# Key weight blocks 2 to 5 of the first stage, each loaded in two or more transfers cut along the partitions

## The chip, the cores and the metric

The kernel runs on one core of one Trainium2 chip. The metric is the device time of one execution in microseconds (us); the time of a kernel is the median of its runs. Engines are named as the profile names them: PE is TensorE (PEld its weight loads), DVE is VectorE, ACT is ScalarE, POOL is GpSimd, SP is SyncE, which here only issues transfers.

## The reference: what is computed

A transformer block with adaptive layer norm, linear attention of 32 heads and a SwiGLU feed-forward part. There are 2048 rows of 1024 features in bf16; the feed-forward width is 3584.

```python
mod = (_silu(c) @ w_mod).reshape(c.shape[0], 6, 1, -1)      # sa, ca, ga, sb, cb, gb
h = _layernorm(x) * (1 + ca) + sa
q, k, v = split(h @ wqkv)                                   # 32 heads of 32
pq, pk = phi(q), phi(k)                                     # where(t > 0, t + 1, exp(t)) + 1e-6
o = (pq @ (pk^T v)) / (pq @ sum(pk) + 1e-6)                 # per head
x = x + ga * (o @ wo)
h = _layernorm(x) * (1 + cb) + sb
x = x + gb * ((silu(h @ w_gate) * (h @ w_up)) @ w_down)
```

## The kernel before

The 2048 rows are worked in four chunks of 512, each chunk four tiles of 128 rows. A contraction over 1024 features is eight matmuls, one for each block of 128 features; the block is numbered `cc`, 0 to 7. The order of the instructions is written out by hand (`manual_schedule`), so what stands here is the order in which each engine's queue gets its work.

The change lies in the **first stage**, in which nothing is yet on the chip. Chunk 0 is normalized and transposed into `M4`, the vectors `sa` and `ca` of the modulation are computed, and the keys of chunk 0 are computed: eight groups (four row tiles by two halves of 512 columns), each of which adds up eight blocks in a bank of PSUM of its own. All this waits on its weights, and the order of the loads and the order of the matmuls are made for each other:

- The loads all go through SP's queue, in this order: four tiles of x (`load_x`, L137); the modulation weights for feature blocks 0 and 1 (`load_wme(0, ...)`, L144, two transfers); key weight blocks 0 and 1 (`load_wk(0, 2)`, L147); modulation weights for blocks 2 to 4 (four transfers); key blocks 2, 3, 4, one transfer each (256 KB: 128 partitions with one row of 2 KB each); modulation weights for blocks 5 to 7 (four transfers); key block 5; key blocks 6 and 7 in one transfer of 512 KB. After them come the value and query weights (`load_cols`, L150) and the x tiles 4 to 7. ACT's queue holds only the 2 KB of `c` here.
- Transfers are counted on eight completion semaphores, reused in turn, so an issue waits until the transfer eight before it has landed.
- PE runs block by block over all groups (`kblk`, with `kmm` at L273, and `kmm7` at L387 for the eighth group, whose bank it shares with the modulation), so that each weight block is used by eight groups once it has landed. Between them are the modulation's matmuls (`mod_mm`, L372, one column each), and `warm` and `fill` (L197, L382), matmuls on zeros that do no work of the reference.
- Once a phase of the modulation is complete (`mod_finish`, L378), DVE scales and shifts the feature blocks of that phase (`modulate`, L255), which PE then uses as weights.
- For blocks 5, 6 and 7 the order turns: PE goes group by group, with blocks 5, 6, 7 of each, and the finished group is evacuated (`k_evac`, ACT L268 and DVE L269, L270).

After the first stage come the value groups of chunk 0 (L288), the queries (L296), the key-value products (L305), the later chunks, the attention output and the feed-forward part (L561, L567, L586), all of which are streams of matmuls that share the five banks in turn.

Of the kernel before, what the change touches and what calls it, by code (L numbers as in the profile page):

```python
# [21 lines left out]
def kernel(  # L22
# [13 lines left out]
    nc = tc.nc  # L36
    P = nc.NUM_PARTITIONS
    _, S, D = A_x.shape
# [23 lines left out]
    wqkv_v = A_wqkv.rearrange("(c p) n -> p c n", p=P)  # L62
# [24 lines left out]
    def view(region, off, shape, dtype=BF16):  # L87
        n = 1
        for s_ in shape:
            n *= s_  # L90
        w = n * (2 if dtype == F32 else 1)
        ap = region[:, off:off + w]
        if dtype == F32:
            ap = ap.bitcast(F32)
        if len(shape) == 2:
            ap = ap.rearrange("p (a b) -> p a b", a=shape[0])
        elif len(shape) == 3:
            ap = ap.rearrange("p (a b c) -> p a b c", a=shape[0], b=shape[1])
        return ap

    wk = view(M12, 0, [DC, D])
# [39 lines left out]
    def load_wme(p, j0, j1):  # L141
        for base in (D, 0):
            s_ = slice(base + PH[p][0] * P, base + PH[p][1] * P)
            nc.sync.dma_start(out=wme[:, j0:j1, s_], in_=wm_v[:, j0:j1, s_])  # L144

    def load_wk(c0, c1):
        nc.sync.dma_start(out=wk[:, c0:c1, :], in_=wqkv_v[:, c0:c1, D:2 * D])  # L147

    def load_cols(dst, base, h):
        nc.sync.dma_start(out=dst[:, :, h * NB:(h + 1) * NB],  # L150
# [2 lines left out]
    for st in range(STC):  # L153
        load_x(st)
    load_wme(0, 0, DC)
    load_wk(0, 2)
    load_wme(1, 0, 4)
    load_wme(1, 4, 8)
    load_wk(2, 3)
    load_wk(3, 4)  # L160
    load_wk(4, 5)
    load_wme(2, 0, 4)
    load_wme(2, 4, 8)
    load_wk(5, 6)
    load_wk(6, 8)


# [577 lines left out]
```

## Time and profile before

| | |
|---|---|
| median of 7 runs | 838.6 us (837.83 to 840.85) |
| profiled execution | 840.85 us, of which the span from the first to the last instruction is 838.8 us |
| granted TensorE clock over the span | 0.998 |
| PE busy | 833.5 us (99% of the span) |
| DVE, ACT, POOL busy | 350.4, 151.6, 80.1 us |
| DMA | 129.41 MB, mean 154 GB/s |
| DMA in the first 12 us, in 12.04 to 20.95, in 20.95 to 26.68 | 272, 342, 357 GB/s |

All durations come from one profiled execution. Matmuls are pipelined: the profile shows 379 ns for one of 512 columns, but in a stream one starts every 0.216 us (64 in 13.81 us). A time "from issue to landing" counts from the issuing instruction's start to the last of the transfer's completions. In lists of waits and chains a name such as `PE bank L273` is engine, tile written and line; `DMA M<-in_A_wqkv_dram` is a transfer from that input to the region of SBUF called M.

### The profile page before, as it was taken

What the parts mean: (1) busy time and instruction counts of PE and PEld (TensorE: products, weight loads), DVE (VectorE), ACT (ScalarE), POOL (GpSimd) and SP (SyncE); (2) the same over time, 40 slices, a digit from 0 to 9 for tenths busy, and PEclk for the clock granted to TensorE, in tenths of its full rate; (3) what the DMA queues carried; (4) which work ended last, traced back from release to release, by engine and by line L of the source; (5) the groups of instructions that cost most, each with busy time, mean ns of one, the idle gap of its engine ahead of it and who ended that gap; (6) DMA issues with size and microseconds to landing.
All of it is one profiled execution on the core that took longest, in us unless ns stands there. A gap on an engine that the chain in (4) does not pass through costs nothing.

```text
span 838.8 us, 10625 instructions
## 1 busy us (share of the span) xinstructions
PE 833.5 (99%) x4232; PEld 390.6 (47%) x4232; DVE 350.4 (42%) x653; ACT 151.6 (18%) x288; POOL 80.1 (10%) x149
## 2 busy tenths in 40 slices
PE   9999999999999999999999999999999999999998
PEld 5444444544444444444444444444444444444445
DVE  5658888788655655344552111111101211111101
ACT  4335533323211111111110001111000111100000
POOL 2124210022122323100000000000000000000000
PEclk9999999999999999999999999999999999999999
DMA  9985879056499898998884215555322555211220
GB/s 302 300 178 102 161 140 250 17 151 135 126 226 226 217 203 226 249 284 238 251 247 136 76 70 150 151 152 153 106 72 84 156 155 153 76 36 46 76 70 26
DMA packets 230545, 129.41 MB, mean 154 GB/s; under 512 B 87648, under 2 KB 216672, under 8 KB 230496
## 3 DMA queue, kind: packets, MB, share of 16 engines
q1 hardware_dynamic: 180144, 97.01, 42.4%
q10 hardware_dynamic: 48048, 23.34, 12.8%
q0 software_dynamic: 2304, 8.39, 2.6%
q8 instruction: 33, 0.54, 0.3%
q14 instruction: 16, 0.13, 0.1%
HBM read 95.42 MB, written 12.58 MB: 129 GB/s over the span
## 4 chain that ended last, share of the span: by engine, by line
PE 96%; DMA 2%; SPq 1%; issue 0%; DVE 0%
PE bank L586 23%; PE bank L567 23%; PE bank L561 23%; PE bank L288 7%; PE bank L518 7%; PE bank L296 7%; PE bank L273 6%; PE bank L491 1%; DMA M<-in_w_mod_dram 1%; PE bank L305 1%; DMA M<-in_A_wqkv_dram 1%; SPq L147 1%; SPq L144 0%; SPq L137 0%; PE bank L387 0%
## 5 line engine op out<-in xcount | busy, mean ns | idle before, releaser
L567 PE MATMUL bank<-M,M 128*128 128x512 bf16 x896 | 211.7, 379 | 0.0
L561 PE MATMUL bank<-M,M 128*128 128x512 bf16 x896 | 211.6, 379 | 0.0
L569 DVE TENSOR_TENSOR M<-bank,e 128x512 bf16<-128x512 f32 x112 | 77.4, 691 | 250.4 <-PE bank L567 246.0
L586 PE MATMUL bank<-M,M 128*128 128x512 bf16 (+2 forms) x728 | 148.0, 363 | 0.0
L564 ACT ACTIVATE e<-bank 128x512 f32<-128x512 f32 x112 | 66.8, 597 | 439.6 <-PE bank L561 403.5
L586 PEld LDWEIGHTS <-M 128*128 128x128 bf16 x952 | 90.9, 98 | 102.9
L567 PEld LDWEIGHTS <-M 128*128 128x128 bf16 x896 | 87.6, 98 | 105.8
L561 PEld LDWEIGHTS <-M 128*128 128x128 bf16 x896 | 87.3, 98 | 103.9
L589 DVE TENSOR_TENSOR M<-bank,M 128x512 bf16<-128x512 f32 (+2 forms) x34 | 22.4, 660 | 169.9 <-PE bank L586 169.9
L273 PE MATMUL bank<-M,M 128*128 128x512 bf16 x248 | 58.1, 387 | 0.7 <-DMA M<-in_A_wqkv_dram 0.5
L518 PE MATMUL bank<-M,M 128*128 128x512 bf16 x256 | 57.9, 379 | 0.0
L296 PE MATMUL bank<-M,M 128*128 128x512 bf16 x256 | 57.5, 379 | 0.0
L288 PE MATMUL bank<-M,M 128*128 128x512 bf16 x256 | 55.9, 379 | 0.0
L268 ACT ACTIVATE e<-bank 128x512 f32<-128x512 f32 x64 | 37.8, 596 | 89.8 <-PE bank L296 52.8
L586 PE MATMUL bank<-M 128*128 128x512 bf16 x224 | 51.0, 379 | 0.0
L270 DVE SCALAR_TENSOR_TENSOR M<-bank,e 128x512 bf16<-128x512 f32 x64 | 44.3, 692 | 4.3 <-DVE e L269 0.5
L328 DVE CUSTOM_DVE_ANT_0 M<-M,sc_bc 128x1024 f32<-128x1024 bf16 x32 | 40.0, 1250 | 0.5
L288 PEld LDWEIGHTS <-M 128*128 128x128 bf16 x256 | 25.0, 98 | 30.0
L518 PEld LDWEIGHTS <-M 128*128 128x128 bf16 x256 | 24.9, 98 | 29.8
L269 DVE TENSOR_SCALAR e<-e 128x512 f32<-128x512 f32 x64 | 28.3, 442 | 24.9 <-ACT e L268 24.6
L273 PEld LDWEIGHTS <-M 128*128 128x128 bf16 x248 | 24.1, 99 | 30.1 <-issue 2.7
L296 PEld LDWEIGHTS <-M 128*128 128x128 bf16 x256 | 24.6, 98 | 27.9
(75 smaller groups left out, 347.5 us busy)
## 6 DMA issues: line engine op xcount, KB each, us to landing
M<-in_B_w_gate_dram SPq DMA_DIRECT2D x56, 512.0 KB, 3.8
M<-in_B_w_up_dram SPq DMA_DIRECT2D x56, 512.0 KB, 4.9
x_scratch<-M POOLq DMA_DIRECT2D x16, 512.0 KB, 5.7
M<-x_scratch ACTq DMA_DIRECT2D x16, 512.0 KB, 3.4
M<-in_B_w_down_dram SPq DMA_DIRECT2D x6, 1024.0 KB, 7.8
M<-in_A_x_dram SPq DMA_DIRECT2D x16, 256.0 KB, 4.5
M<-in_A_wqkv_dram SPq DMA_DIRECT2D x4, 1024.0 KB, 11.3
M<-in_A_x_dram ACTq DMA_DIRECT2D x16, 256.0 KB, 3.8
```

Source lines behind the costliest of these rows:

```text
L268: nc.scalar.activation(out=e[:], in_=acc, func=ACT.Exp)
L270: nc.vector.scalar_tensor_tensor(out=dst, in0=acc, scalar=0.0, in1=e[:], op0=ALU.max, op1=ALU.add)
L273: nc.tensor.matmul(acc[:], lhsT=M4[:, sc_, cc, t * P:(t + 1) * P], rhs=wk[:, cc, h * NB:(h + 1) * NB], start=(cc == 0), stop=(cc == DC - 1))
L288: nc.tensor.matmul(acc[:], lhsT=M4[:, sc_, cc, t * P:(t + 1) * P], rhs=wv[:, cc, h * NB:(h + 1) * NB], start=(cc == 0), stop=(cc == DC - 1))
L296: nc.tensor.matmul(acc[:], lhsT=wq[:, cc, qc * P:(qc + 1) * P], rhs=M4[:, sc_, cc, :], start=(cc == 0), stop=(cc == DC - 1))
L328: nc.vector.tensor_tensor_reduce(out=prod.rearrange("p (j k) -> p j k", j=DC), in0=rowT[i][:, :, b, :], in1=sc_bc[:].rearrange("p (j k) -> ...
L518: nc.tensor.matmul(acc[:], lhsT=oTs[st % 3][:, cc, :], rhs=wo[:, cc, hs], start=(cc == 0), stop=(cc == DC - 1))
L561: nc.tensor.matmul(g_ps[:], lhsT=wg_blk[:, cc, fs], rhs=M4[:, sc_, cc, :], start=(cc == 0), stop=(cc == DC - 1))
L564: nc.scalar.activation(out=sg[:], in_=g_ps[:], func=ACT.Silu)
L567: nc.tensor.matmul(u_ps[:], lhsT=wu_blk[:, cc, fs], rhs=M4[:, sc_, cc, :], start=(cc == 0), stop=(cc == DC - 1))
L569: nc.vector.tensor_tensor(out=gus[sc_][:, f, :], in0=u_ps[:], in1=sg[:], op=ALU.mult)
L586: nc.tensor.matmul(y_ps[:, 0:w], lhsT=gus[sc_][:, f, t * P:(t + 1) * P], rhs=wd(f)[:, c0:c1], start=(f == 0), stop=(f == FC - 1))
```

## The change

`load_wk` gets a list of partition cuts and issues one transfer for each piece. Key blocks 2, 3 and 4 are loaded as partitions 0 to 119 and 120 to 127, two transfers each; block 5 as 0 to 119, 120 to 123, 124 and 125, 126, and 127, five transfers. That is seven transfers more on SP's queue; the bytes, their places and the order of the blocks stay. Blocks 0, 1, 6 and 7 and all other loads stay as they are.

```diff
-    def load_wk(c0, c1):
-        nc.sync.dma_start(out=wk[:, c0:c1, :], in_=wqkv_v[:, c0:c1, D:2 * D])
+    def load_wk(c0, c1, cuts=(0, P)):
+        for p0, p1 in zip(cuts[:-1], cuts[1:]):
+            nc.sync.dma_start(out=wk[p0:p1, c0:c1, :], in_=wqkv_v[p0:p1, c0:c1, D:2 * D])
...
     load_wk(0, 2)
     load_wme(1, 0, 4)
     load_wme(1, 4, 8)
-    load_wk(2, 3)
-    load_wk(3, 4)
-    load_wk(4, 5)
+    load_wk(2, 3, (0, 120, P))
+    load_wk(3, 4, (0, 120, P))
+    load_wk(4, 5, (0, 120, P))
     load_wme(2, 0, 4)
     load_wme(2, 4, 8)
-    load_wk(5, 6)
+    load_wk(5, 6, (0, 120, 124, 126, 127, P))
     load_wk(6, 8)
```

## The prediction

> **What bounds the kernel now.** First the page: how busy TensorE is and what the chain that ended last consists of.
>
> ```profile
> span 838.8 us, 10625 instructions
> PE 833.5 (99%) x4232; PEld 390.6 (47%) x4232; DVE 350.4 (42%) x653; ACT 151.6 (18%) x288; POOL 80.1 (10%) x149
> PE 96%; DMA 2%; SPq 1%; issue 0%; DVE 0%
> ```
>
> TensorE sets the time, except for 3% of the span in which the chain goes through transfers and their issue. The second view, the chain in order of time, cut to the end of the first stage, shows where that is: it sits on transfers until 26.64 us, and from there on TensorE works without a gap, so whatever moves the moment 26.68 moves the end by as much.
>
> ```profile
> 15.23 1.39 SPq L144
> ...
> 16.66 3.32 SPq L147
> ...
> 20.02 6.62 DMA M<-in_A_wqkv_dram
> 26.64 0.04 issue
> 26.68 6.16 PE bank L273 x20
> ```
>
> The transfer that ends it is key blocks 6 and 7 (512 KB, `load_wk(6, 8)`), issued at 20.02. Third, the issues with their time to landing, asked for around the issue of each key block (the SP queue's timeline gives the issue times 9.80, 11.72, 12.20, 16.66, 20.02, in this order):
>
> ```profile
> M<-in_A_wqkv_dram SPq DMA_DIRECT2D x1, 256.0 KB, 7.2
> ...
> M<-in_A_wqkv_dram SPq DMA_DIRECT2D x1, 256.0 KB, 7.5
> ...
> M<-in_A_wqkv_dram SPq DMA_DIRECT2D x1, 256.0 KB, 7.7
> ...
> M<-in_A_wqkv_dram SPq DMA_DIRECT2D x1, 256.0 KB, 8.6
> ...
> M<-in_A_wqkv_dram SPq DMA_DIRECT2D x1, 512.0 KB, 6.6
> ```
>
> Blocks 2, 3, 4 follow each other in one queue and land at 17.0, 19.2 and 19.9. Block 4 came 0.70 after block 3, which is the pace of 256 KB; block 3 came 2.2 after block 2, so 1.5 us were lost there. The DMA view of 16.4 to 17.7 has the only other traffic:
>
> ```profile
> q1 hardware_dynamic: 467, 0.45, 101.7%
> q8 instruction: 1, 0.02, 5.3%
> ```
>
> One packet of 16 KB of instructions, and 5.3% of 16 engines over 1.3 us is one engine for 1.1 us. The completions in the trace say the same. Each transfer counts 16 engines. For block 2 all 16 are in by 16.99; for block 3 fifteen are in by 17.68 and the last at 19.17; for blocks 6 and 7 fifteen by 25.12 and the last at 26.64. So one engine of sixteen has been 1.5 us behind since the instruction packet, and every transfer of this stage ends with it.
>
> Fourth, the windows, cut where the clock records change:
>
> ```profile
> 19.89:23.30 3.41, 3.13 (x36) 1.64 (x34) 0.00 (x0) 0.00 (x0) 0.00 (x0) 1.00 1.07 343
> 23.30:26.72 3.42, 2.35 (x35) 1.25 (x35) 1.59 (x5) 0.00 (x0) 0.00 (x0) 1.00 1.08 361
> 26.72:30.13 3.41, 3.41 (x9) 1.18 (x9) 1.81 (x5) 1.19 (x2) 0.00 (x0) 0.50 1.07 376
> ```
>
> The fourth number is TensorE's busy time, the third from the end the granted clock. After the stretch in which TensorE waited most, the clock is halved for 3.41 us, on the chain: 3.41 x 0.5 = 1.7 us.
>
> **The change part by part.** *Bytes.* A block is 128 rows of 2 KB, 8 rows for each of 16 engines; 0.70 us for 8 rows is 0.087 us a row. The last 8 partitions are exactly one engine's share. No row shows a transfer of 120 partitions. Its bounds: 15 engines with 8 rows each and one with none, or all 16 as now, or fewer engines with more rows. I take the first, since 8 rows an engine is the nearest row; the others are rivals. The Trainium skill ("DMA: Bandwidth & Descriptors", how many engines k) says that the number of engines is the largest up to 16 that divides the outermost size, lowest numbers first, with 100 partitions on 10 as its example; 120 would run on engines 0 to 14. No run here shows it.
>
> If the skipped engine is the late one, it loses 4 x 8 = 32 rows, 2.8 us of work against 1.5 us of lag, and is last no more. Next is the fifteenth, 25.12, plus the rows it takes over: one from each of three blocks (0.26 us) up to seven if one engine also gets a row of each of block 5's four pieces (0.61). Blocks 6 and 7 then land between 25.4 and 25.7; I take 25.5, near the lower end because most engines get three rows or fewer. TensorE resumes at 25.54 instead of 26.68: **1.1 us**.
>
> *What is late next.* Block 6's matmuls also need its rows modulated by VectorE, which follows the last modulation weights. These land 1.5 us earlier by the same engine, and TensorE's three waits for them vanish: 0.42, 0.22 and 0.50 us by start times (21.9 to 22.32, 23.28 to 23.49, 24.10 to 24.60), 1.1 in all. Block 6's weight load, which waited for VectorE until 26.08, is ready at 24.9, block 7's modulation ends 25.2 instead of 26.36. The transfer stays last, by some 0.3 us.
>
> *Issues.* Seven more transfers; an unblocked issue on SP takes 0.43 us (11.72 and 12.20), together 3.0. SP was blocked in this stretch anyway: 1.87 - 0.43 at block 2, 3.32 - 0.43 at block 5, 4.3 together. These issues move past blocks 6 and 7, the value and query weights and four x tiles on SP. Each waits on the transfer eight before it (lanes are reused in turn), so the six issues ahead of blocks 6 and 7 hold fewer bytes in flight: theirs then waits for the second piece of the last modulation group, 20.8 by the other fifteen engines. Packets of the first x tile start 1.0 us after its issue (0.73 to 1.76), and the two blocks need 1.4: any issue before 25.5 - 2.4 = 23.1 costs nothing. Beyond that it costs its whole delay. The extra completion waits on TensorE's queue, at most seven, fall before blocks that have landed: nothing to 0.3 us, taken as nothing, as TensorE then waits for blocks 6 and 7 anyway.
>
> A rule speaks against all this. Row: the 2 KB load of c took 2.9 us from issue to landing beside the x tiles, and blocks 3 and 4 landed 0.70 apart although each took 7.5: such latency overlaps. The same page (Rules for kernel authors) advises against splitting over partitions, wants one 128-partition transfer, and puts about 2 us on each small one; seven of them in series would add 14 us by it, against none by the row.
>
> *Clock.* In the stretch 23.30 to 26.72 TensorE streamed 32% of the columns that a full clock passes (512 in 0.216 us); three earlier stretches that kept the clock had 67 to 69%. Resuming at 25.54 adds 1.14 us of dense matmuls, 33% more: 65%, about what kept it. So in the profiled execution 1.7 us more would go. That execution took 840.85 us, the slowest of the seven; the median of 838.6 is 2.25 below and may not carry this loss whole. Bounds 0 and 1.7; I take **1.1**, nearer to the one execution with a row. The skill ("TensorE: Matmul & The Clock Gate", Part 1) calls the window free-running, so that the loss would vary between executions; the trace shows its edges 3.41 us apart, in one execution only.
>
> Sum in the profiled execution: 840.85 - 1.1 - 1.7 = 838.0. For the median: 838.6 - 1.1 - 1.1 = **836.4**, with 835.8 to 837.7 for this case.
>
> **Rivals.** *The late engine is another one.* The completions don't name it. If it is not skipped, it stays last and gets 0 to 7 rows more, 0 to 0.61 us, and the clock may be lost in more executions (0 to 0.85): 838.6 to 840.1, about 839.1. Against it: a fetch that always hits one engine sits more likely at an end of the row than in the middle; that is a guess.
>
> *Fewer engines for 120 rows (slower).* With 8 engines of 15 rows each, four blocks put 28 rows more on them: 2.4 us. Landing moves to 27.5 if the late engine is not among them, 29.1 if it is: +0.9 to +2.4, and up to 0.85 of clock: 839.5 to 841.9, about 840.9. It decides from 10 engines down (12 rows, 16 extra, 1.4 us, eats the 1.5 gained). For it: no row shows 120. Against: nothing in the rows favours 8.
>
> *Nothing moves.* All sixteen engines still carry 120 rows between them, or the lag is small in executions without the profiler: 838.3 to 838.9, about 838.6.
>
> **How the numbers follow.** Forecast 0.66, another engine late 0.18, fewer engines 0.10, nothing moves 0.06. 0.2% is 1.7 us, about what a measurement of this kernel can tell from no change: bounds 836.9 and 840.3. Of the forecast's 0.66 some 0.53 lies below 836.9. Slower: 0.10 from fewer engines, 0.03 from the other late engine with all its costs. Same: 0.34. Range 835.6 to 839.8: the forecast whole, and most of the two middle rivals.
>
> **What would show it.** Right: block 3 lands 0.7 to 0.8 after block 2, TensorE resumes after blocks 6 and 7 near 25.5, no half clock after it, blocks 6 and 7 issued before 23. Wrong: one completion of blocks 6 and 7 still 1.5 us after the others (another engine); blocks 3 and 4 more than 1 us apart with several late completions (fewer engines); an issue of blocks 6 and 7 after 23.1 (SP).

## The result, and the profile after

The change makes the kernel slower: median 840.76 us (15 runs, 840.03 to 842.68) against 838.53 (35 runs of the kernel before, 837.66 to 840.85). The ratio is 1.0027, 95% interval 1.0020 to 1.0033. Forecast were 836.4 and a range of 835.6 to 839.8.

The profiled execution took 842.12 us, 1.27 more than that of before, which ran part of its time at half clock and was the slowest of its 35 executions; so the two profiles show 1.3 of the 2.2 us. The page and its chain:

```profile
span 840.1 us, 10639 instructions
PE 834.0 (99%) x4232; PEld 390.8 (47%) x4232; DVE 350.7 (42%) x653; ACT 151.5 (18%) x288; POOL 79.8 (9%) x149
PE 96%; DMA 2%; SPq 1%; issue 0%; DVE 0%
```

Nothing of this shows the loss; the chain in order of time does, at the end of the first stage (lines after the change are one higher: L148 is `load_wk`, L274 the key matmuls, L289 the value matmuls):

```profile
16.41 5.63 DMA M<-in_w_mod_dram
22.05 0.02 issue
22.06 5.20 DMA M<-in_A_wqkv_dram
27.26 0.04 issue
27.30 6.80 PE bank L274 x20
34.10 0.93 PE bank L388 x11
```

Key blocks 6 and 7 are issued at 22.06 instead of 20.02 and land at 27.26 instead of 26.64. The twenty matmuls behind them then take 6.80 us instead of 6.16. Both together are the 1.3 us by which the span grew. From the first value matmul (L289) to the end it takes 805.2 us in both kernels, so all of the difference arises before.

The windows, cut at the clock records of this execution, show why those matmuls take longer (fourth number: PE busy; third from the end: granted clock):

```profile
18.37:21.78 3.41, 3.41 (x21) 1.63 (x20) 0.00 (x0) 0.00 (x0) 0.00 (x0) 1.00 1.10 311
21.78:25.20 3.42, 2.32 (x51) 1.50 (x50) 0.00 (x0) 0.00 (x0) 0.00 (x0) 1.00 1.03 277
25.20:28.61 3.41, 3.01 (x19) 1.00 (x18) 1.83 (x5) 0.26 (x1) 0.00 (x0) 0.50 1.08 348
28.61:32.02 3.41, 3.41 (x10) 1.20 (x9) 2.68 (x6) 1.53 (x3) 0.00 (x0) 0.50 1.06 376
```

Two stretches at half clock instead of one. And the last number of each line, the rate of the transfers in GB/s, is lower than before: 277 while block 5's pieces are on their way, where the kernel before had 343 to 361. The same view of 15.5 to 18.5, when blocks 2 to 4 are on their way, of the kernel before and then of the changed one:

```profile
15.50:18.50 3.00, 2.98 (x41) 1.80 (x40) 1.22 (x4) 0.00 (x0) 0.00 (x0) 1.00 1.07 360
```

```profile
15.50:18.50 3.00, 2.61 (x38) 1.57 (x36) 1.22 (x4) 0.00 (x0) 0.00 (x0) 1.00 1.04 270
```

The share in which the 16 DMA engines are busy (the number before the rate) is as full as before (1.07, 1.04), yet they move a quarter less. Packet by packet, in each microsecond from 15 to 19 one of 2 KB took a median of 84 to 87 ns before and 102 to 129 after. The engines work slower; they are not idle. No rival had that.

### The profile page after: what moved, and what is told of

Same layout as the page of the kernel before. It is cut to its first block, busy times and chain, and to the rows that moved or that the text cites. A ratio compares the mean times of both kernels' runs of the same rounds, so it can differ in the third digit from the quotient of the medians.

```text
span 840.1 us, 10639 instructions
## 1 busy us (share of the span) xinstructions
PE 834.0 (99%) x4232; PEld 390.8 (47%) x4232; DVE 350.7 (42%) x653; ACT 151.5 (18%) x288; POOL 79.8 (9%) x149
## 4 chain that ended last, share of the span: by engine, by line
PE 96%; DMA 2%; SPq 1%; issue 0%; DVE 0%
PE bank L587 23%; PE bank L568 23%; PE bank L562 23%; PE bank L289 7%; PE bank L519 7%; PE bank L297 7%; PE bank L274 6%; DMA M<-in_w_mod_dram 2%; PE bank L492 1%; PE bank L306 1%; DMA M<-in_A_wqkv_dram 1%; SPq L144 0%; SPq L148 0%; SPq L137 0%; PE bank L388 0%
## 5 line engine op out<-in xcount | busy, mean ns | idle before, releaser
L274 PE MATMUL bank<-M,M 128*128 128x512 bf16 x248 | 59.1, 392 | 0.4 <-DMA M<-in_A_wqkv_dram 0.4
L289 PE MATMUL bank<-M,M 128*128 128x512 bf16 x256 | 55.9, 379 | 0.0
L289 PEld LDWEIGHTS <-M 128*128 128x128 bf16 x256 | 25.0, 98 | 30.0
L274 PEld LDWEIGHTS <-M 128*128 128x128 bf16 x248 | 24.4, 100 | 30.6 <-issue 3.5
```

Source lines behind the costliest of these rows:

```text
L274: nc.tensor.matmul(acc[:], lhsT=M4[:, sc_, cc, t * P:(t + 1) * P], rhs=wk[:, cc, h * NB:(h + 1) * NB], start=(cc == 0), stop=(cc == DC - 1))
L289: nc.tensor.matmul(acc[:], lhsT=M4[:, sc_, cc, t * P:(t + 1) * P], rhs=wv[:, cc, h * NB:(h + 1) * NB], start=(cc == 0), stop=(cc == DC - 1))
```

## The experiments

The theories at the start: (1) rows of a cut block move slower, be it because of fifteen engines or of the cut itself; (2) seven more transfers through eight reused completion lanes hold up SP; (3) block 5's one-row pieces pile up on one engine; (4), added later, only the mixture with small pieces is slow; (5) all of it arrives as later blocks 6 and 7 and a lost clock.

**Blocks 2 to 4 alone.**

```diff
-    load_wk(5, 6, (0, 120, 124, 126, 127, P))
+    load_wk(5, 6)
```

> Blocks 2 to 4 cut as 120 and 8 partitions, block 5 whole (three transfers more than before; the changed kernel has seven and is 2.2 us slower than before by its median). Theory 1, slow rows: while 120-row pieces are in flight, a 2 KB packet takes 102 to 129 ns instead of 84 to 88, some 0.3 us more for each cut block; three of four blocks give 0.9 us later landing of blocks 6 and 7 and +1.0 to +1.8 us on the time, the upper end with a lost clock window. Theory 2, lanes: the cost comes from seven more transfers through eight reused completion lanes; three of seven, at most +1.0 us, and less if only the four around blocks 6 and 7 count. Theory 3, single rows: block 5's one-row pieces queue on one engine (0.22 us each) and are the cost; here no change or a gain of up to 1 us.

Median 840.29 us, ratio to before 1.0020 (1.0011 to 1.0029): most of the loss. The rate in 15.5 to 18.5 is 235 GB/s. (The loads of the changed kernel moved 270, 254 and 235 in this window in three kernels that have them, and those of four kernels with blocks 2 to 4 whole (before, block 5 alone, seven tiny transfers, block 5's matmuls moved) 356 to 364; so differences among the cut kernels are not read further.) Theory 3 expected no loss here, and theory 2 allowed at most 1.0 us, so neither is the main cause.

**Block 5 alone.**

```diff
-    load_wk(2, 3, (0, 120, P))
-    load_wk(3, 4, (0, 120, P))
-    load_wk(4, 5, (0, 120, P))
+    load_wk(2, 3)
+    load_wk(3, 4)
+    load_wk(4, 5)
```

> Only block 5 cut, in five pieces (120, 4, 2, 1, 1 partitions). Theory 1, slow rows: one block of four, +0.3 to +0.6 us. Theory 2, lanes: four of the seven transfers, right ahead of blocks 6 and 7, +1.2 to +2.2 us, with blocks 6 and 7 issued at 22 instead of 20. Theory 3, single rows: the whole cost, about +2 us, with one engine ending blocks 6 and 7 last, after 25.6.

839.19 us, 1.0009 (1.0000 to 1.0017). In executions at full clock, 839.19 against 838.31 for before: +0.9; blocks 2 to 4 at full clock gave 839.46, +1.15. The two parts add up to 2.0. Block 5's loss has two possible sources that this run doesn't separate. The packets slow down (2 KB ones take medians of 113 to 135 ns in 22 to 23 us), and the engines run dry, in the same stretch and again in 24.5 to 25.5:

```profile
22.00:25.00 3.00, 2.45 (x58) 1.89 (x58) 0.12 (x1) 0.00 (x0) 0.00 (x0) 1.00 0.84 245
```

That blocks 6 and 7 are issued at 21.55 only may be why; no run tests it. The one-row pieces land at 24.20 and 24.45, two and four rows at 23.80 and 23.99: 0.2 to 0.25 us for each piece on one queue, as theory 3 says, but they did not end the stage; blocks 6 and 7 did, at 26.46, by the last of two engines that were already behind at block 4 (its completions: fourteen by 17.84, then 18.75 and 19.16).

**Sixteen engines, uneven cut.** Blocks 2 to 5 each as partitions 0 to 111 and 112 to 127.

```diff
-    load_wk(2, 3, (0, 120, P))
+    load_wk(2, 3, (0, 112, P))
...
-    load_wk(5, 6, (0, 120, 124, 126, 127, P))
+    load_wk(5, 6, (0, 112, P))
```

> Blocks 2 to 5 each cut as 112 and 16 partitions, so that all sixteen engines can share both pieces evenly (7 rows and 1 row); four transfers more than before. Theory 1, slow rows on fifteen engines: packets of 2 KB stay at 84 to 88 ns and the time within 0.5 us of before. Theory 1b, the cutting itself slows the rows (an 8-row run on each engine is broken): packets over 100 ns and +1 to +2 us. Theory 2, lanes: four of seven transfers, +1.0 to +1.3 us.

840.72 us, 1.0028 (1.0017 to 1.0039): as slow as the change, with sixteen completions for each piece, so with no engine left out. Packets of 2 KB took 119 to 149 ns, and the rate fell to 256 GB/s:

```profile
15.50:18.50 3.00, 1.80 (x34) 1.20 (x33) 0.98 (x4) 0.00 (x0) 0.00 (x0) 1.00 1.07 256
```

So it is not that one engine is missing. The cut is enough.

**Seven tiny transfers.** Whole blocks, and seven loads of 16 bytes where the change has its seven.

```diff
+    def tiny(*ns):
+        for n in ns:
+            nc.sync.dma_start(out=junk[0:1, 8 * n:8 * n + 8], in_=c[:, 8 * n:8 * n + 8])
...
     load_wk(2, 3)
+    tiny(0)
...
     load_wk(5, 6)
+    tiny(3, 4, 5, 6)
     load_wk(6, 8)
```

> Blocks 2 to 5 whole as before; seven transfers of 16 bytes each to an unused tile at the places where the change adds its seven. Nothing of the weights' shapes changes. Theory 2, lanes and issues: the whole cost, about +2 us, with blocks 6 and 7 issued at 22 instead of 20. Theory 1 (slow rows) and theory 3 (single rows of 2 KB on one engine): within 0.4 us of before.

838.08 us, 0.9998 (0.9989 to 1.0007): nothing, though blocks 6 and 7 are issued at 21.13. Theory 2 falls. The issue came before the prediction's bound of 23.1; whether one as late as 23.1 would still be free was not tested, and with block 5 alone, where it came at 21.55, the engines ran partly dry.

**Equal halves.** Blocks 2 to 4 as 0 to 63 and 64 to 127.

```diff
-    load_wk(2, 3, (0, 120, P))
+    load_wk(2, 3, (0, 64, P))
...
```

> Blocks 2 to 4 cut as 64 and 64 partitions, block 5 whole: the same three transfers more as with 120 and 8 (which cost 1.9 us by the medians, 2 KB packets 120 to 150 ns). Theory 1b, any transfer of other than 128 partitions is written slower: packets of 2 KB over 100 ns and +1 to +2 us. Theory 1c, only uneven cuts are slow (112 and 120 are no multiple of 64): packets at 84 to 90 ns, time within 0.5 us of before. Theory 4, small pieces: the 8- and 16-partition pieces interleave badly; with 64 and 64 no cost.

839.74 us, 1.0018 (1.0009 to 1.0027), 269 GB/s, packets 111 to 119 ns. An even cut is slow as well.

```profile
15.50:18.50 3.00, 2.18 (x32) 1.11 (x30) 1.22 (x4) 0.00 (x0) 0.00 (x0) 1.00 1.04 269
```

**Transfers one kind at a time.** 21 loads, and then larger ones, queued behind blocks 6 and 7 where they disturb no key block. First 256 KB and less:

```diff
     load_wk(6, 8)
...
+    for n in (128, 120, 112, 96, 64):
+        for i in range(3):
+            nc.sync.dma_start(out=spare[k][0:n], in_=wqkv_v[0:n, k % 8, 2 * D:3 * D])
+            k += 1
...
+    for n in (128, 120):
+        for i in range(3):
+            nc.sync.dma_start(out=copy[i * P:i * P + n, :], in_=wqkv_v[0:n, k % 8, 2 * D:3 * D])
...
```

> The kernel before with 21 extra transfers queued after blocks 6 and 7, into room that is unused then: three each of 128, 120, 112, 96 and 64 partitions of 2 KB rows into SBUF, then three each of 128 and 120 rows into a DRAM scratch. They delay the value weights by some 10 us, so its total time says nothing; only the landings count. At the pace of whole blocks 256 KB take 0.70 us. Theory 1b, writing SBUF in other than 128 partitions is slow: 120 and 112 take 0.9 to 1.1 us each, and DRAM copies of 128 and 120 rows differ by no more than one row in nine. Theory 4, only the mixture with small pieces is slow: 120 and 112 take 0.62 to 0.72 us. If reading rows of HBM in another order is slow, the DRAM copies of 120 are slow too.

By the first of their completions whole blocks followed each other every 0.67 to 0.70 us and those of 120 partitions every 1.0 us, though these are 16 KB smaller and no small piece is among them; packets 125 to 135 ns. Those of 112 and 96 partitions took 0.9 and 0.8 us, where the pace of whole blocks would give 0.6 and 0.5. That rules out theory 4. For the DRAM copies, which were to show whether reading the rows is slow, the test failed: issued too slowly, they left the engines partly idle (share 0.68 to 0.80). So once more with 480 and 512 KB, and with 64 partitions in two placements:

```diff
...
+    for n, i in ((128, 0), (128, 2), (120, 4), (120, 6)):
+        nc.sync.dma_start(out=m4[0:n, i:i + 2, :], in_=wqkv_v[0:n, i:i + 2, vcol])
+    for i in (0, 4):
+        nc.sync.dma_start(out=m6[0:64, i:i + 4, :], in_=wqkv_v[0:64, i:i + 4, vcol])
+    for i in (0, 4):
+        nc.sync.dma_start(out=m4[0:P:2, i:i + 4, :], in_=wqkv_v[0:64, i:i + 4, vcol])
...
```

> The kernel before with 12 extra transfers of 480 or 512 KB behind blocks 6 and 7, so that the engines do not run dry between them: two each of 128 partitions, 120 partitions, 64 neighbouring partitions, 64 partitions with a step of two, and DRAM copies of 128 and of 120 rows. Total time says nothing; the landings and the packets do. Where whole transfers take 1.4 us each: if the writing side of SBUF is what slows the cut ones, 120 partitions take about 2.0 us, 64 neighbouring ones over 1.7, 64 with a step of two are faster than the neighbouring ones, and DRAM copies of 120 rows keep 2 KB packets of 84 to 90 ns. If the reading side is: the DRAM copies of 120 rows are slow too.

Its windows, for whole blocks, mostly 120 partitions, mostly 64 neighbouring ones, and 64 with a step of two together with the first DRAM copies of 128 rows:

```profile
24.00:25.70 1.70, 1.07 (x16) 0.51 (x15) 1.27 (x5) 0.00 (x0) 0.00 (x0) 1.00 1.05 388
28.80:30.80 2.00, 2.00 (x14) 1.06 (x13) 1.93 (x5) 1.74 (x4) 0.00 (x0) 1.00 1.07 240
35.00:37.00 2.00, 0.00 (x0) 0.00 (x0) 0.69 (x1) 0.00 (x0) 0.00 (x0) 0.84 1.03 178
40.10:41.60 1.50, 0.00 (x0) 0.00 (x0) 0.00 (x0) 0.00 (x0) 0.00 (x0) 0.50 1.05 397
```

The engines are full in all four. The same 64 rows read from HBM reach 178 GB/s into 64 neighbouring partitions and, in a window shared with the first DRAM copies, 397 into every second one. By last completions 512 KB took 2.5 to 2.8 us in the one and 1.0 to 1.3 in the other. The reading side is the same, so for 64 partitions it is where the rows land. (The DRAM copies of 120 rows kept a median of 84 ns a packet while they ran, but again did not fill the engines, so for 120 partitions the reading side is not excluded.)

**The test in place.** Blocks 2 to 4 as the even and the odd partitions.

```diff
+    def load_wk2(c0, c1):
+        for i in range(2):
+            nc.sync.dma_start(out=wk[i:P:2, c0:c1, :], in_=wqkv_v[i:P:2, c0:c1, D:2 * D])
...
-    load_wk(2, 3)
+    load_wk2(2, 3)
...
```

> Blocks 2 to 4 each in two transfers of 64 partitions, the even ones and the odd ones, block 5 whole: as many transfers, rows and bytes as with 0 to 63 and 64 to 127 (1.2 us slower than before at the same clock, 2 KB packets 111 to 119 ns). Placement theory: what slows a cut load is that its rows land in few neighbouring partitions at a time; here each transfer is spread over all 128, so the packets stay at 84 to 95 ns and the time within 0.4 us of before. Number-of-pieces theory (two transfers of 4 rows an engine instead of one of 8): +1.2 us again.

838.84 us against 838.70, 1.0005 (0.9994 to 1.0015): no loss to be seen, with as many transfers, rows and bytes as the equal halves.

```profile
15.50:18.50 3.00, 2.98 (x46) 1.85 (x43) 1.22 (x4) 0.00 (x0) 0.00 (x0) 1.00 1.06 356
```

By time alone the two intervals (this one and that of the equal halves) overlap; the rate, 356 against 269, and the packets, 84 to 88 ns against 111 to 119, keep them apart. With the probe before it, the placement theory is shown, for 64 partitions.

**Which engine is late.** Block 3 cut as 98 and 30 partitions, block 4 as 104 and 24, block 5 as 88 and 40, block 2 whole.

> Which engine is late. Block 3 is cut as 98 and 30 partitions, block 4 as 104 and 24, block 5 as 88 and 40, block 2 whole. By the completion counts of the runs so far a transfer uses the largest number of engines up to 16 that divides its partitions, so these use 14, 15, 13, 12, 11 and 10 engines. If they are the lowest-numbered ones, the engine that the instruction packet delays shows as a last completion some 1 us after the others in every transfer that reaches it and in none that stops before. The prediction's reading: it is the sixteenth, so no cut transfer has it. The change's own trace (120 partitions late by 0.86 us, 8 partitions not) says one of the ninth to fifteenth: late in those with 15 engines, and down to some number.

Beside those that come at once, the transfers have 14, 15, 13, 12, 11 and 10 completions, so these many engines carry them. In this execution the instruction packet starts at 15.79. Last completion and the one before: 98 partitions 18.76 and 17.88; 30: 19.07 and 18.18; 104: 20.00 and 19.19; but 24: 19.47 and 19.38. The late engine has rows of the 104 partitions, which 13 engines share, and none of the 24, which 12 share. If the lowest-numbered engines are used, as the Trainium skill says ("DMA: Bandwidth & Descriptors", how many engines k), it is the thirteenth. The change's own trace fits: in block 3 the 120 partitions end 0.86 us late (18.04, 18.90), the last 8 partitions, on eight engines, all by 17.87.

**The clock.** The changed kernel with 30 more matmuls on zeros at the two waits; they compute nothing of the reference.

```diff
     mod_mm(2, 0, 4, 8)
-    fill(6)
+    fill(22)
...
             kblk((g,), cc)
+            if g == 0 and cc == 5:
+                fill(14)
```

> The changed kernel with 30 more matmuls on zeros (112 columns, 49 ns each) at the two places where TensorE waits for the last modulation weights and for blocks 6 and 7; they do no work of the reference and leave all transfers alone. Clock theory: the change's extra waits drop TensorE below what keeps the clock in most executions (granted clock below 1.0 in 14 of 16, against 11 of 56 listed for before), which costs 1 to 1.7 us each time; with the filling the clock stays at 1.0 in most and the median falls by 0.6 to 1.5 us, to 839.3 to 840.2. If the clock has no part in it: no change, or slower by what the filling takes, up to 0.5 us.

840.15 us, and the clock stays at 1.0 in 10 of 11 executions. That is 0.6 us below the change, and 1.8 above the kernel before of the same set, against 2.2: 0.4 to 0.6 us are the clock. The change's own two executions at full clock took 840.03 and 840.88. At full clock this kernel takes 840.14, the kernel before 838.32 in the same set.

**Work to cover the wait.** The kernel before, and the changed one, with the matmuls of block 5 moved ahead for all eight groups.

```diff
     kblk(range(6, 8), 4)
+    kblk(range(8), 5)
     for g in range(8):
-        for cc in range(5, 8):
+        for cc in range(6, 8):
```

> The kernel before, all loads unchanged; only the matmuls of key block 5 for all eight groups are moved ahead of the grouped ones of blocks 6 and 7, so that TensorE has 1.7 us of work at hand when block 5 has landed (25.3) and no longer waits 0.5 us for blocks 6 and 7 (26.64). If the wait on the last transfer and the halved clock after it are what the first stage loses: 0.5 to 0.9 us faster in executions without a halved clock, up to 2.5 us in those with one; median -0.7 to -1.5. If ScalarE and VectorE, which evacuate the groups, are late instead: no gain.

> The changed kernel with the same move of block 5's matmuls. Theory 5, the change's cost reaches the end only as a later landing of blocks 6 and 7 plus a halved clock: with 1.7 us of work in between, most of its 2.2 us goes, and it stands 0 to 0.8 us above before. If the cost is spread over the stage (modulation weights landing later as well): it keeps +1 us or more over the kernel with the move alone.

On the kernel before it gives 837.78 against 838.56, 0.9990 (0.9981 to 0.9998): a version faster than both; at full clock it is 837.73 against 838.28. TensorE runs without a gap from 25.74, although blocks 6 and 7 land at 26.58 in that execution:

```profile
25.74 1.69 PE L273 MATMUL bank<-M,M 128*128 128x512 bf16 x7
27.26 0.33 PE L387 MATMUL bank<-M,M 128*128 128x384 bf16 x1
27.42 3.19 PE L273 MATMUL bank<-M,M 128*128 128x512 bf16 x14
```

On the changed kernel it gives 840.52, 2.7 us above the kernel with the move alone. Much of that is the clock, which 9 of its 11 executions lost and 1 of 11 of the other; in the two at full clock it is 839.4, 1.7 above. Theory 5 as I had put it falls: with blocks 6 and 7 covered, the wait before block 5 still starts the matmuls later (26.18 instead of 25.74) and still costs the clock (half from 26.27 on). In the changed kernel without the move TensorE waits 1.01 us before 25.08 for the last modulation weights, in the kernel before 0.34 us before 24.60:

```profile
25.08 0.47 PE L373 MATMUL bank<-scT,M 128*128 128x1 bf16 x12 [1.01 <-DMA M<-in_w_mod_dram]
```

With the move the same wait is 0.94 us:

```profile
24.88 0.45 PE L373 MATMUL bank<-scT,M 128*128 128x1 bf16 x12 [0.94 <-DMA M<-in_w_mod_dram]
```

Rows that follow a cut block in the queues arrive later too, and no work of block 5 can start before they have.

## Why the prediction was wrong

- **Where the time is decided: right.** The first value matmul comes 805.2 to 805.5 us before the end in all twelve kernels that kept the loads behind it, so the first stage alone decides.
- **"8 rows an engine is the nearest row", at 0.087 us a row: this step failed.** The count was right: the completions of the 120 partitions are one at once and fifteen later, those of 8, 4, 2 and 1 partitions 8, 4, 2 and 1. The price was not: 120 partitions took 1.0 us, not 0.70. I bounded how many engines carry the rows and never what a row costs when its neighbours land elsewhere; the only row for it was of whole blocks. The Trainium skill has a rule for half spans, on a page that I did not weigh ("SBUF — State Buffer", Door 1): partitions 0 to 63 reach only half of the 16 ports through which transfers write. The 178 GB/s of neighbouring partitions, against 388 of whole blocks, agree with that. But by the table there 120 and 112 partitions reach all 16 ports, so the rule does not explain the change's own pieces. That these are slow is measured; why stays open.
- **The rule that spoke against the change** was weighed against latency, and the tiny transfers show that latency and issues cost nothing, as I had it. But its advice, one transfer over 128 partitions, was right for another reason, and for pieces of neighbouring partitions only: even and odd halves cost nothing measurable.
- **"If the skipped engine is the late one": it is not.** In the changed kernel a 120-partition piece still has one late completion (18.90 after 18.04). If the lowest-numbered engines are used, the late one is the thirteenth, and the change skips the sixteenth. The guess about the ends of the row had no basis. Even with the right engine the forecast 1.1 us would have stood against 2.0 us of slower rows.
- **The lag of 1.5 us is not there in every execution.** Four profiled executions have the loads of before up to blocks 6 and 7. Between the last two completions of these lay 1.5 us in that of before and 1.5 with block 5's matmuls moved, but 0.6 and 0.3 in the two probes.
- **The clock: wrong sign.** I put a loss of 1.1 us into the median of before. Of 88 executions of it in four sets with their clocks listed, 74 had the full clock (median 838.37; 839.89 for thirteen of the others). There was nothing to win in the median; the change lost the clock in 14 of the 16 executions listed. The condition was too strict as well: 65% of the columns was taken as about what keeps the clock. Counted the same way in eleven traces (without the two probes and the filled kernel), of the first nine 3.41 us stretches after the first clock record, those at full clock went on at half clock after 26 to 32% (six of them) and at full clock after 37% or more.
- **SP and VectorE: right in that neither decided**, in the trace of the change and with seven tiny transfers; with block 5 alone a later issue may have let the engines run dry.
- **The rival "fewer engines"** named 840.9 and the result is 840.8, but not for its reason: fifteen engines carried the rows. Of the sign named for it the first half came, blocks 3 and 4 more than 1 us apart (18.90 and 19.92), but with one late completion and not several. That the size came out is chance: more rows on an engine, as the rival had it, and slower rows, as measured, happen to cost about the same.

The sum by the runs: blocks 2 to 4 +1.15 and block 5 +0.9 us at full clock, 2.0 together; the filled kernel's 840.14 against 838.32 gives 1.8 for the same; and the lost clock brings the median to +2.2, 0.4 to 0.6 of which the filling takes back.

## What to carry to other kernels

A transfer's price per byte belongs to its shape. Before a load is cut along the partitions, look for a transfer of that very shape, not only for the bytes of each engine; full engines with fewer GB/s in the windows is how the cost looks. And if TensorE waits for the last of a row of transfers, order the matmuls so that it has work that needs only what has landed: that gave 0.8 us here (0.55 at full clock) without touching a load.

## What was not expected of the hardware

- Three blocks in two transfers of 64 partitions each cost 1.2 us (medians) as lower and upper halves, and nothing measurable as even and odd partitions.
- The packets of another load in the queues slow down beside a cut one: 768-byte packets of the modulation weights took a median of 53 ns at 18 to 19 us in the changed kernel, 39 before.
- A 16 KB packet of instructions occupies one engine for 1.0 to 1.4 us in the first stage of all these traces. In block 3 behind it the last completion came 1.5 us after the others in the kernel before (17.68, 19.17) and 0.9 in the changed one (18.04, 18.90).
